# Two edits to a fused attention and two-MLP kernel: partial sums of the first MLP kept in memory, and a priority for four activations

## The chip, the cores and the metric

The kernel runs on one core of one Trainium2 chip. The metric is device time in microseconds (us) of one execution; the kernel before ran three times, 584.2, 585.54 and 586.94 us, so its median is 585.54 us. Lower is better. Engines are named as the profile does: PE is TensorE (matrix products), PEld its weight loads, DVE is VectorE, ACT is ScalarE, POOL is GpSimd, SP is SyncE, whose queue issues most of the DMAs.

## What is computed

A decaying linear attention over 2 batches of 768 positions, 8 heads of 64, gives x of 1536 tokens by 512. Two MLPs follow, each 512 to 2048 to 512; the first squares a ReLU, the second uses a leaky ReLU:

```
x = attention(q, k, v, lam)            # 1536 x 512
h = np.maximum(x @ w_in, 0.0)
x = h * h @ w_out                      # first MLP
h = x @ w2_in
g = np.maximum(0.01 * h, h)
out = g @ w2_out                       # second MLP
```

Inputs to the attention are float32. The MLP weights come as 64-bit floats.

## The kernel before, in words

**Precision by splitting.** Each MLP operand is split into a high part and a low part (`split`, `converting`, `activate`), and a product is three matrix products: high by high, high by low, low by high (`three`). Weights arrive as raw 64-bit words in `raw` (two buffers of 1 MB), and `converting` turns one such piece into a high and a low tile by steps on ACT (lines 109 and 128) and DVE (lines 110 to 130). A generator hands out one conversion step at a time between groups of products.

**Tiling and stages.** The 1536 tokens are three token tiles of 512, t = 0, 1, 2. The 2048 hidden features are cut into four pieces of 512, so each MLP l (0 or 1) has four stages s. In a stage, `first` computes the hidden features of one token tile (four blocks m of 128, 12 products each) and `activate` makes their high and low parts, `g0h`/`g0l` for t = 0, `g1h`/`g1l` for t = 1. `second` then multiplies them by the second weight matrix: four output blocks m per token tile, 12 products each, into one of eight PSUM banks.

**The pair group.** In the second MLP, token tiles 0 and 1 are done together by `first_pair`: a seven-product scheme in place of eight. Its operands are differences of token halves (`token_sums`, which writes tiles `t2`, `t3`, `t4`) and of weight halves (`weight_sums`). Per half h of the stage it runs the seven products; `plus` (line 507) adds up their results on DVE under a raised priority of 400, and `put` hands the four finished blocks of each token tile to `activate` (lines 441 to 443: two ACT operations and one DVE subtraction that writes the low part). After `first_pair`, PE goes on with `second(1, s, 0)`, which reads `g0h` and `g0l`, block by block: products 1 to 3 need block 0, 4 to 6 block 1, and so on.

**Partial sums.** Each output block gets one contribution from each of the four stages. In the first MLP they are added up on the chip in `acc[t]`, one tile of 128 x 4 x 512 for each token tile: a copy on ACT in stage 0 (line 575), an add on DVE in stages 1 and 2 (line 585), and an add in stage 3 that gives the result (line 578, or 585 for t = 2), which is split into `xhi`, `xlo`. These three tiles carry the tags t2, t3 and t4, which `token_sums` uses again for its own tiles; so a tile of `token_sums` can be written only when the `acc` tile of that tag has been read for the last time, and `acc[2]` is read until the end of the first MLP. In the second MLP they are added up in device memory: a copy on ACT into a buffer `f` (line 591), a plain DMA to `spill` in stage 0, an adding DMA issued by POOL in stages 1 and 2 (line 601), and in stage 3 the sum is loaded back and added to the last contribution on DVE (line 594). Buffers `f` come from a pool of nine (`plain`), which `activate`, `first_pair` and `token_sums` use as well.

**What sets the order.** The order on PE is the program's (a manual schedule). The orders on ACT, DVE, POOL and SP are set by a scheduler at build time, which takes the program's order and the priorities that `tc.high_priority` gives. Each engine and each queue works its list strictly in order: an instruction that waits holds all behind it.

Of the kernel before, what the change touches and what calls it, by code (L numbers as in the profile page):

```python
# [9 lines left out]
F32 = mybir.dt.float32  # L10
# [4 lines left out]
ALU = mybir.AluOpType  # L15
P = 128
# [3 lines left out]
def tile_retention_then_two_mlps(  # L20
# [12 lines left out]
    nc = tc.nc  # L33
    B, H, S, D = q.shape
    NT, DM = out.shape
# [4 lines left out]
    TT = 512  # L40
    NTILE = NT // TT
# [8 lines left out]
    dram = ctx.enter_context(tc.tile_pool(name="dram", bufs=1, space=bass.MemoryType.DRAM))  # L50
# [10 lines left out]
    def plain():  # L61
        return fp.tile([P, TT], F32, tag="f", name="f")

    def dma(dst, src):
        return nc.sync.dma_start(dst, src)  # L65

    def split(hi, lo, src):
        nc.scalar.copy(hi, src)
        nc.vector.tensor_tensor(out=lo, in0=src, in1=hi, op=ALU.subtract)
# [81 lines left out]
    xhi = [None] * NTILE  # L151
    xlo = [None] * NTILE

    def new_x(t):
        xhi[t] = xp.tile([P, KD, TT], F32R, tag=f"xhi{t}", name=f"xhi{t}")
        xlo[t] = xp.tile([P, KD, TT], F32R, tag=f"xlo{t}", name=f"xlo{t}")
# [233 lines left out]


    late = ctx.enter_context(tc.tile_pool(name="late", bufs=1, reuse_waits="tile"))
    spill = [[dram.tile([P, DM], F32, name=f"spill{t}{m}") for m in range(4)] for t in range(NTILE)]
    spilled = {}
    g, acc, x0f, x1f, tt = {}, [None] * NTILE, {}, {}, {}

    def new_g(t, first_stage=False):
        if first_stage and t == 2:
            tags = ("sw0", "sw1")
        else:  # L400
            tags = (f"g{t % 2}h", f"g{t % 2}l")
        g[t] = [late.tile([P, KF, TT], F32R, tag=tag, name=tag) for tag in tags]
# [32 lines left out]
    def activate(l, src, r, ghi, glo):  # L435
        if l == 0:
            nc.scalar.activation(r, src, AF.Relu)  # L437
            nc.scalar.square(ghi, r)
            nc.scalar.square(r, r)  # L439
        else:  # L440
            nc.scalar.activation(ghi, src, AF.Prelu, alpha=0.01)
            nc.scalar.activation(r, src, AF.Prelu, alpha=0.01)
        nc.vector.tensor_tensor(out=glo, in0=r, in1=ghi, op=ALU.subtract)  # L443
# [25 lines left out]
    def first_pair(s):  # L469
        new_g(0)  # L470
        new_g(1)
        ve = nc.vector
        w = {}
        for h in range(2):
            hi, lo = wts[1, s, 0, h]
            for i in range(2):
                for j in range(2):
                    w[h, f"A{i + 1}{j + 1}"] = [x[:, 2 * j:2 * j + 2, i * P:(i + 1) * P] for x in (hi, lo)]
            for n in range(4):
                w[h, f"S{n + 1}"] = [sums[s, h][:, part, n] for part in range(2)]  # L480
        x = {
            "B11": (xhi[0][:, 0:2], xlo[0][:, 0:2]),
            "B21": (xhi[0][:, 2:4], xlo[0][:, 2:4]),
            "B22": (xhi[1][:, 2:4], xlo[1][:, 2:4]),
            "T1": (xhi[1][:, 0:2], xlo[1][:, 0:2]),
        }
        for n in (2, 3, 4):
            x[f"T{n}"] = (tt[n][:, 0], tt[n][:, 1])
        ps, s1, s2, r22 = {}, {}, {}, {}

        def product(h, where, a, b, start=True):
            if start:
                ps[h, where] = bank()
            (ah, al), (bh, bl) = w[h, a], x[b]
            ops = []
            for j in range(2):
                ops += [(ah[:, j], bh[:, j]), (ah[:, j], bl[:, j]), (al[:, j], bh[:, j])]
            three(ps[h, where], ops, start, True, not start)
            return ps[h, where]

        def put(h, src, r, i, t):
            m = 2 * h + i
            activate(1, src, r, g[t][0][:, m], g[t][1][:, m])

        def plus(h, out, where, other):
            with tc.high_priority(offset=400):
                ve.tensor_tensor(out=out, in0=ps[h, where], in1=other, op=ALU.add)

        both = range(2)
        for h in both:  # L510
            b = product(h, "A", "A11", "B11")
            s1[h] = plain()
            nc.scalar.copy(s1[h], b)
            yield True
        for h in both:
            product(h, "B", "S2", "T2")
            s2[h] = plain()
            plus(h, s2[h], "B", s1[h])
            yield True
        for h in both:  # L520
            product(h, "D", "A22", "T4")
            yield True
        for h in both:
            product(h, "C", "S1", "T1")
            yield True
        for h in both:
            product(h, "B", "S3", "T3", False)
            plus(h, s1[h], "B", s1[h])
            r22[h] = plain()
            plus(h, r22[h], "C", s1[h])  # L530
            plus(h, s1[h], "D", s1[h])
            yield False
        for h in both:
            put(h, product(h, "A", "A12", "B21", False), plain(), 0, 0)
            put(h, s1[h], s1[h], 1, 0)
            yield False
        for h in both:
            product(h, "C", "S4", "B22", False)
            plus(h, s2[h], "C", s2[h])
            yield False  # L540
        for h in both:
            put(h, r22[h], r22[h], 1, 1)
            put(h, s2[h], s2[h], 0, 1)

    def second(l, s, t, ms=range(4)):
        last = s == NS - 1
        groups = [(m, slice(0, DM)) for m in ms]
        if (l, s, t) == (1, NS - 1, NTILE - 1):
            groups[-1:] = [(3, slice(0, DM // 2)), (3, slice(DM // 2, DM))]
        for m, cs in groups:  # L550
            if l == 0 and m == 0:
                if s == 0:
                    acc[t] = late.tile([P, 4, 512], F32, tag=f"t{t + 2}", name=f"acc{t}")
                if last:
                    new_x(t)
            if l == 1 and last and cs.start == 0:
                spilled[m] = plain()
                dma(spilled[m], spill[t][m])
            ghi, glo = g[t]
            ms_ = slice(m * P, (m + 1) * P)  # L560
            ops = []
            for kk in range(KF):
                hi, lo = (x[:, kk % 2] for x in wts[l, s, 1, kk // 2])
                if l == 0:
                    ops += [(hi[:, ms_], ghi[:, kk]), (hi[:, ms_], glo[:, kk]), (lo[:, ms_], ghi[:, kk])]
                else:
                    ops += [(ghi[:, kk, ms_], hi[:, cs]), (ghi[:, kk, ms_], lo[:, cs]), (glo[:, kk, ms_], hi[:, cs])]
            ps = bank()[:, cs]
            three(ps, ops[:6], True, False)
            yield  # L570
            three(ps, ops[6:], False, True)
            if l == 0:
                a = acc[t][:, m]
                if s == 0:
                    nc.scalar.copy(a, ps)
                elif last and t < 2:
                    f = plain()
                    nc.vector.tensor_tensor(out=f, in0=ps, in1=a, op=ALU.add)
                    (x0f, x1f)[t][m] = f
                    if t == 0 or m > 1:  # L580
                        split(xhi[t][:, m], xlo[t][:, m], f)
                    if t == 1 and m > 1:
                        token_sums(m - 2)
                else:
                    nc.vector.tensor_tensor(out=a, in0=ps, in1=a, op=ALU.add)
                    if last:
                        split(xhi[t][:, m], xlo[t][:, m], a)
            else:
                if not last:
                    spilled[m] = plain()  # L590
                    nc.scalar.copy(spilled[m], ps)  # L591
                else:
                    a = spilled[m][:, cs]
                    nc.vector.tensor_tensor(out=a, in0=ps, in1=a, op=ALU.add)
                if last:
                    r0 = t * TT + m * P
                    dma(out[r0:r0 + P, cs], spilled[m][:, cs])
                elif s == 0:
                    dma(spill[t][m], spilled[m])
                else:  # L600
                    nc.gpsimd.dma_start(spill[t][m], spilled[m], accum_op=ALU.add)  # L601
            if t == 2 and m == 3:
                i = stages.index((l, s))
                opened.update((*stages[n], 1, h) for n, h in ((i + 1, 1), (i + 2, 0)) if n < len(stages))
            yield not (l == 0 and last and t == 1 and m > 1)
# [49 lines left out]
```

## Time and profile before

| | |
|---|---|
| median of three runs | 585.54 us |
| profiled execution, its own time | 584.32 us |
| its span, first to last instruction | 582.5 us |
| PE busy | 571.4 us, 98% of the span, 3099 instructions |
| PEld busy | 476.1 us, 82% |
| DVE busy | 405.1 us, 70%, 565 instructions |
| ACT busy | 277.0 us, 48%, 425 instructions |
| POOL busy | 46.6 us, 8%, 61 instructions |
| moved by DMA | 59.75 MB, 103 GB/s in the mean |

The profile gives each group of instructions its busy time and the idle time of its engine just before it, with the engine that released it. The ends of matrix products are modelled and overlap their successors, so times between starts tell more on PE than busy time. A timeline lists instructions in order of time, equal neighbours merged (x2, x3); the bracket at the end of a row is the idle time before it and its releaser. In tile names of the profile the buffer numbers are left out: `t` stands for t2, t3 and t4, `raw<-in_moe_w_in` for the first and the second MLP's weights alike. A name such as SPq is the issuing queue of an engine.

### The profile page before, as it was taken

What the parts mean: (1) busy time and instruction counts of PE and PEld (TensorE: products, weight loads), DVE (VectorE), ACT (ScalarE), POOL (GpSimd) and SP (SyncE); (2) the same over time, 40 slices, a digit from 0 to 9 for tenths busy, and PEclk for the clock granted to TensorE, in tenths of its full rate; (3) what the DMA queues carried; (4) which work ended last, traced back from release to release, by engine and by line L of the source; (5) the groups of instructions that cost most, each with busy time, mean ns of one, the idle gap of its engine ahead of it and who ended that gap; (6) DMA issues with size and microseconds to landing.
All of it is one profiled execution on the core that took longest, in us unless ns stands there. A gap on an engine that the chain in (4) does not pass through costs nothing.

```text
span 582.5 us, 7802 instructions
## 1 busy us (share of the span) xinstructions
PE 571.4 (98%) x3099; PEld 476.1 (82%) x3099; DVE 405.1 (70%) x565; ACT 277.0 (48%) x425; POOL 46.6 (8%) x61
## 2 busy tenths in 40 slices
PE   6999999999999999999999979999999999999997
PEld 6888888888888888888888858888888888888886
DVE  3789999949248752969768999929874787316222
ACT  2344698537361661528537473633662475325110
POOL 3426000000000000000000000000203111220000
PEclk9899999999999999999999999999999999999999
DMA  8999432443104040122201215262339424562432
GB/s 175 236 206 205 159 122 95 153 136 98 47 0 132 14 145 0 61 85 73 72 1 41 82 46 191 70 214 81 45 101 237 83 60 55 69 94 55 161 110 91
DMA packets 60148, 59.75 MB, mean 103 GB/s; under 512 B 38984, under 2 KB 40272, under 8 KB 60112
## 3 DMA queue, kind: packets, MB, share of 16 engines
q1 hardware_dynamic: 56128, 52.71, 30.0%
q0 software_dynamic: 3456, 6.29, 7.9%
q8 instruction: 24, 0.39, 0.3%
q10 hardware_dynamic: 528, 0.26, 0.2%
q14 instruction: 12, 0.10, 0.1%
HBM read 46.66 MB, written 12.59 MB: 102 GB/s over the span
## 4 chain that ended last, share of the span: by engine, by line
PE 95%; DMA 2%; DVE 1%; issue 1%; SPq 0%; ACT 0%; POOL 0%; ACTq 0%; POOLq 0%
PE ps L447 88%; PE ps L268 2%; PE ps L285 2%; PE ps L336 2%; DMA raw<-in_moe_w_in 1%; PE ps L334 1%; PE ps L309 1%; DMA q<-in_q 1%; SPq L65 0%; DVE g0l L443 0%; ACT qT L272 0%; POOL kd L303 0%; DVE hb L120 0%; DVE rb L117 0%; PE ps L259 0%
## 5 line engine op out<-in xcount | busy, mean ns | idle before, releaser
L447 PE MATMUL ps<-xhi,w1h 128*128 128x512 f32 x288 | 112.1, 389 | 0.0
L447 PE MATMUL ps<-xlo,w1h 128*128 128x512 f32 x288 | 112.0, 389 | 0.0
L447 PE MATMUL ps<-xhi,w1l 128*128 128x512 f32 x288 | 112.0, 389 | 0.0
L447 PEld LDWEIGHTS ps<-xhi,w1l 128*128 128x128 f32 x288 | 54.1, 188 | 11.3
L447 PEld LDWEIGHTS ps<-xhi,w1h 128*128 128x128 f32 x288 | 54.1, 188 | 11.2 <-issue 0.2
L447 PEld LDWEIGHTS ps<-xlo,w1h 128*128 128x128 f32 x288 | 54.1, 188 | 11.2
L443 DVE TENSOR_TENSOR g0l<-f,g0h 128x512 fp32r<-128x512 f32 x60 | 41.0, 688 | 26.3 <-ACT f L439 14.9
L601 POOL DMA_DIRECT2D spill<-f x24 | 21.7, 903 | 437.0 <-ACT f L591 437.0
L447 PE MATMUL ps<-w2h,g0l 128*128 128x512 f32 (+1 forms) x132 | 50.8, 385 | 3.1 <-DVE g0l L443 3.1
L130 DVE TENSOR_TENSOR w2l<-hb,w2h 128x1024 fp32r<-128x1024 f32 x16 | 19.6, 1224 | 47.4 <-ACT w2h L128 47.2
L447 PE MATMUL ps<-w2l,g0h 128*128 128x512 f32 (+1 forms) x132 | 50.5, 383 | 0.0
L447 PE MATMUL ps<-w2h,g0h 128*128 128x512 f32 (+1 forms) x132 | 50.5, 383 | 0.0
L437 ACT ACTIVATE f<-ps 128x512 f32<-128x512 f32 x48 | 28.5, 593 | 39.5 <-PE ps L447 39.5
L591 ACT COPY f<-ps 128x512 f32<-128x512 f32 x36 | 21.1, 587 | 53.4 <-PE ps L447 51.2
L109 ACT ACTIVATE hb<-raw 128x1024 f32<-128x1024 f32 x32 | 36.8, 1154 | 16.6 <-DMA raw<-in_moe_w_in 5.6
L447 PE MATMUL ps<-g0h,w2h 128*128 128x512 f32 x112 | 43.6, 389 | 0.0
L447 PE MATMUL ps<-g0l,w2h 128*128 128x512 f32 x112 | 43.6, 389 | 0.0
L447 PE MATMUL ps<-g0h,w2l 128*128 128x512 f32 x112 | 43.6, 389 | 0.0
L117 DVE SCALAR_TENSOR_TENSOR rb<-raw,rb 128x1024 f32<-128x1024 uint32 x32 | 39.1, 1222 | 0.4
L120 DVE TENSOR_TENSOR hb<-hb,rb 128x1024 f32<-128x1024 f32 x32 | 39.1, 1222 | 0.3
L113 DVE SCALAR_TENSOR_TENSOR hb<-raw,hb 128x1024 uint32<-128x1024 uint32 x32 | 39.1, 1222 | 0.3
L128 ACT CAST w2h<-hb 128x1024 fp32r<-128x1024 f32 x16 | 16.9, 1054 | 39.2 <-PE ps L447 37.3
(125 smaller groups left out, 1106.4 us busy)
## 6 DMA issues: line engine op xcount, KB each, us to landing
raw<-in_moe_w_in SPq DMA_DIRECT2D x16, 1024.0 KB, 5.6
raw<-in_moe_w_out SPq DMA_DIRECT2D x16, 1024.0 KB, 4.8
spill<-f POOLq DMA_DIRECT2D x24, 256.0 KB, 4.3
k<-in_k SPq DMA_DIRECT2D x12, 256.0 KB, 4.9
q<-in_q SPq DMA_DIRECT2D x12, 256.0 KB, 5.1
v<-in_v SPq DMA_DIRECT2D x12, 256.0 KB, 4.9
spill<-f SPq DMA_DIRECT2D x12, 256.0 KB, 2.9
f<-spill SPq DMA_DIRECT2D x12, 256.0 KB, 2.8
```

The costliest lines, as they stand in the source:

```text
L109: nc.scalar.activation(hf, w_hi.bitcast(F32), AF.Abs)
L113: yield ve.scalar_tensor_tensor(out=hb, in0=w_hi, scalar=0xC0000000, in1=hb, op0=ALU.bitwise_and, op1=ALU.bitwise_or)
L117: yield ve.scalar_tensor_tensor(out=rf, in0=w_lo, scalar=2.0 ** -52, in1=rf, op0=ALU.mult, op1=ALU.mult)
L120: yield ve.tensor_tensor(out=hf, in0=hf, in1=rf, op=ALU.add)
L128: nc.scalar.copy(hi, hf)
L130: yield ve.tensor_tensor(out=lo, in0=hf, in1=hi, op=ALU.subtract)
L268: nc.tensor.transpose(ps[:, p, :], src[:, 2 * p:2 * p + 2, :].rearrange("s h d -> s (h d)"), ident)
L437: nc.scalar.activation(r, src, AF.Relu)
L443: nc.vector.tensor_tensor(out=glo, in0=r, in1=ghi, op=ALU.subtract)
L447: nc.tensor.matmul(ps, a, b, start=start and n == 0, stop=stop and n == len(ops) - 1, skip_group_check=again)
L591: nc.scalar.copy(spilled[m], ps)
L601: nc.gpsimd.dma_start(spill[t][m], spilled[m], accum_op=ALU.add)
```

## The change

Two edits, as the diff shows. First, the first MLP's partial sums go the way of the second's: stage 0 copies the product to a buffer `f` and writes it to `spill[0]` by a plain DMA, stages 1 and 2 copy it and add it there by an adding DMA of POOL, stage 3 loads the sum into an `f` buffer before the products and adds on DVE in place. The tiles `acc` are gone. Second, in `put` the activations of t = 0 stand under a priority of 400.

```diff
-    spill = [[dram.tile([P, DM], F32, name=f"spill{t}{m}") for m in range(4)] for t in range(NTILE)]
+    spill = [[[dram.tile([P, DM], F32, name=f"spill{l}{t}{m}") for m in range(4)] for t in range(NTILE)]
+             for l in range(2)]
...
             m = 2 * h + i
-            activate(1, src, r, g[t][0][:, m], g[t][1][:, m])
+            with tc.high_priority(offset=400 if t == 0 else 0):
+                activate(1, src, r, g[t][0][:, m], g[t][1][:, m])
...
-            if l == 0 and m == 0:
-                if s == 0:
-                    acc[t] = late.tile([P, 4, 512], F32, tag=f"t{t + 2}", name=f"acc{t}")
-                if last:
-                    new_x(t)
-            if l == 1 and last and cs.start == 0:
+            if l == 0 and last and m == 0:
+                new_x(t)
+            if last and cs.start == 0:
                 spilled[m] = plain()
-                dma(spilled[m], spill[t][m])
+                dma(spilled[m], spill[l][t][m])
...
+            if not last:
+                spilled[m] = plain()
+                nc.scalar.copy(spilled[m], ps)
                 if s == 0:
-                    nc.scalar.copy(a, ps)
-                elif last and t < 2:
-                    f = plain()
-                    nc.vector.tensor_tensor(out=f, in0=ps, in1=a, op=ALU.add)
-                    (x0f, x1f)[t][m] = f
+                    dma(spill[l][t][m], spilled[m])
+                else:
+                    nc.gpsimd.dma_start(spill[l][t][m], spilled[m], accum_op=ALU.add)
+            else:
+                a = spilled[m][:, cs]
+                nc.vector.tensor_tensor(out=a, in0=ps, in1=a, op=ALU.add)
+                if l == 1:
+                    r0 = t * TT + m * P
+                    dma(out[r0:r0 + P, cs], a)
+                elif t == 2:
+                    split(xhi[t][:, m], xlo[t][:, m], a)
+                else:
+                    (x0f, x1f)[t][m] = a
                     if t == 0 or m > 1:
-                        split(xhi[t][:, m], xlo[t][:, m], f)
+                        split(xhi[t][:, m], xlo[t][:, m], a)
                     if t == 1 and m > 1:
                         token_sums(m - 2)
...
```

On PE no instruction moves: its list is the same in both kernels. DVE has 24 instructions fewer (the adds of stages 1 and 2), ACT 24 more (the copies of the same), POOL 24 adding DMAs more, and SP 24 DMAs more (12 writes in stage 0, 12 loads in stage 3). In the changed file line 443 has become 444, 441 and 442 are 442 and 443, and 507 is 509.

**VectorE, the last conversion steps ahead of the end of the first pair group.** `t_2728` is t4; L507 and L509 are the adds of `plus`; the other rows convert weights. Before:

```order
L130 TENSOR_TENSOR w2l<-hb,w2h 128x1024
L69 TENSOR_TENSOR t_2728<-f,t_2728 128x512 x2
L120 TENSOR_TENSOR hb<-hb,rb 128x1024
L110 TENSOR_SCALAR hb<-hb 128x1024
L111 TENSOR_SCALAR hb<-hb 128x1024
L507 TENSOR_TENSOR f<-ps,f 128x512
L130 TENSOR_TENSOR w2l<-hb,w2h 128x1024
```

Now:

```order
L130 TENSOR_TENSOR w2l<-hb,w2h 128x1024
L120 TENSOR_TENSOR hb<-hb,rb 128x1024
L110 TENSOR_SCALAR hb<-hb 128x1024
L111 TENSOR_SCALAR hb<-hb 128x1024
L130 TENSOR_TENSOR w2l<-hb,w2h 128x1024
L113 SCALAR_TENSOR_TENSOR hb<-raw,hb 128x1024
```

The two writes of t4 have left this place for earlier ones, behind the `token_sums` that feed them, and one conversion step (L113) stands ahead of the adds.

**VectorE, the rows that follow: the end of the pair group, where g0l is written for PE.** Before:

```order
L507 TENSOR_TENSOR f<-ps,f 128x512 x4
L113 SCALAR_TENSOR_TENSOR hb<-raw,hb 128x1024
L507 TENSOR_TENSOR f<-ps,f 128x512 x3
L116 TENSOR_SCALAR rb<-hb 128x1024
L443 TENSOR_TENSOR g0l<-f,g0h 128x512
L117 SCALAR_TENSOR_TENSOR rb<-raw,rb 128x1024
L443 TENSOR_TENSOR g0l<-f,g0h 128x512
L120 TENSOR_TENSOR hb<-hb,rb 128x1024
L443 TENSOR_TENSOR g0l<-f,g0h 128x512 x2
L443 TENSOR_TENSOR g1l<-f,g1h 128x512 x4
```

Now:

```order
L509 TENSOR_TENSOR f<-ps,f 128x512 x6
L444 TENSOR_TENSOR g0l<-f,g0h 128x512
L509 TENSOR_TENSOR f<-ps,f 128x512
L116 TENSOR_SCALAR rb<-hb 128x1024
L444 TENSOR_TENSOR g0l<-f,g0h 128x512 x3
L509 TENSOR_TENSOR f<-ps,f 128x512
L117 SCALAR_TENSOR_TENSOR rb<-raw,rb 128x1024
L444 TENSOR_TENSOR g1l<-f,g1h 128x512
L120 TENSOR_TENSOR hb<-hb,rb 128x1024
L444 TENSOR_TENSOR g1l<-f,g1h 128x512 x3
```

Of the conversion steps only L116 stands ahead of or between the four writes of g0l now, and the last add of `plus`, which serves t = 1, stands behind them.

**SyncE's queue, stage 3 of the first MLP.** `raw` is a piece of weights; spill_999 to spill_1010 are the first MLP's twelve blocks in memory, four to a token tile. Before, these five rows followed each other:

```order
L65 DMA raw<-in_moe_w_in 128x4x256 x2
L65 DMA raw<-in_moe_w_out 128x2x512 x2
L65 DMA raw<-in_moe_w_in 128x4x256 x2
L65 DMA raw<-in_moe_w_out 128x2x512
L65 DMA spill_999<-f 128x512
```

Now:

```order
L65 DMA raw<-in_moe_w_out 128x2x512 x2
L65 DMA f<-spill_999 128x512
L65 DMA f<-spill_1000 128x512
L65 DMA f<-spill_1001 128x512
L65 DMA f<-spill_1002 128x512
L65 DMA f<-spill_1003 128x512
L65 DMA f<-spill_1005 128x512
L65 DMA f<-spill_1004 128x512
L65 DMA f<-spill_1006 128x512
L65 DMA f<-spill_1007 128x512
L65 DMA f<-spill_1008 128x512
L65 DMA f<-spill_1009 128x512
```

Twelve loads (the twelfth, spill_1010, follows) stand between the last piece of second weights and the two pieces of first weights for the second MLP's stage 1, which come right behind them. (In the list of before, spill_999 is a block of the second MLP.)

## Rows read from the trace of the kernel before

**Rows 1.** Waits of TensorE: line, what ended them; us in total, times, longest

```profile
PE ps L447 <- DVE g0l L443: 3.1, 3, 1.5
```

**Rows 2.** Busy us (instructions) by engine in two stretches, TensorE clock, DMA share, GB/s

```profile
300.00:350.00 50.00, 46.94 (x205) 37.92 (x204) 46.29 (x65) 32.14 (x50) 0.00 (x0) 1.00 0.17 53
285.00:312.00 27.00, 27.00 (x120) 22.34 (x119) 18.60 (x27) 12.97 (x20) 0.00 (x0) 1.00 0.00 1
```

**Rows 3.** Chain of waits, the piece ahead of the wait: start, us, what

```profile
63.51 280.40 PE ps L447 x1236
```

**Rows 4.** Timeline of TensorE, end of the pair group: start, us, instruction, idle before

```profile
343.73 0.39 PE L447 MATMUL ps<-w2h,g0h 128*128 128x512 f32 x1
...
345.88 0.50 PE L447 MATMUL ps<-w2h,g0l 128*128 128x512 f32 x1 [1.53 <-DVE g0l L443]
...
349.36 0.50 PE L447 MATMUL ps<-w2h,g0l 128*128 128x512 f32 x1 [0.76 <-DVE g0l L443]
...
350.15 0.40 PE L447 MATMUL ps<-w2h,g0l 128*128 128x512 f32 x1
```

**Rows 5.** Timeline of VectorE in the same place and ahead of it

```profile
332.25 1.24 DVE L130 TENSOR_TENSOR w2l<-hb,w2h 128x1024 fp32r<-128x1024 f32 x1
333.38 1.31 DVE L69 TENSOR_TENSOR t<-f,t 128x512 fp32r<-128x512 f32 x2
334.59 1.24 DVE L120 TENSOR_TENSOR hb<-hb,rb 128x1024 f32<-128x1024 f32 x1
...
343.94 0.69 DVE L507 TENSOR_TENSOR f<-ps,f 128x512 f32<-128x512 f32 x1 [0.25 <-PE ps L447]
344.54 0.69 DVE L116 TENSOR_SCALAR rb<-hb 128x1024 uint32<-128x1024 uint32 x1
...
346.88 0.69 DVE L443 TENSOR_TENSOR g0l<-f,g0h 128x512 fp32r<-128x512 f32 x1
```

**Rows 6.** Timeline of ScalarE in the same place

```profile
333.52 1.15 ACT L109 ACTIVATE hb<-raw 128x1024 f32<-128x1024 f32 x1
335.86 1.05 ACT L128 CAST w2h<-hb 128x1024 fp32r<-128x1024 f32 x1 [1.19 <-DVE hb L120]
338.99 1.16 ACT L109 ACTIVATE hb<-raw 128x1024 f32<-128x1024 f32 x1 [2.08 <-DVE w2l L130]
340.04 0.60 ACT L441 ACTIVATE g0h<-ps 128x512 fp32r<-128x512 f32 x1
...
344.03 1.18 ACT L442 ACTIVATE f<-f 128x512 f32<-128x512 f32 x2
```

**Rows 7.** Groups, VectorE, 130:300, first MLP's adds: count, busy us, mean ns, idle

```profile
L585 DVE TENSOR_TENSOR acc<-ps,acc 128x512 f32<-128x512 f32 x24 | 16.5, 689 | 19.8 <-PE ps L447 19.6
```

**Rows 8.** The page's groups, second MLP's copies

```profile
L591 ACT COPY f<-ps 128x512 f32<-128x512 f32 x36 | 21.1, 587 | 53.4 <-PE ps L447 51.2
```

**Rows 9.** Timeline of SyncE's queue, weights: first start, us over both, what

```profile
268.21 10.75 SPq L65 DMA_DIRECT2D raw<-in_moe_w_out  x2
...
316.99 14.60 SPq L65 DMA_DIRECT2D raw<-in_moe_w_in  x2
```

**Rows 10.** DMA issues by line: count, KB each, median us to landing

```profile
raw<-in_moe_w_in SPq DMA_DIRECT2D x16, 1024.0 KB, 5.6
...
f<-spill SPq DMA_DIRECT2D x12, 256.0 KB, 2.8
```

**Rows 11.** Timeline of VectorE, the last stage of the first MLP

```profile
285.35 0.69 DVE L578 TENSOR_TENSOR f<-ps,acc 128x512 f32<-128x512 f32 x1
...
312.17 0.69 DVE L443 TENSOR_TENSOR g0l<-f,g0h 128x512 fp32r<-128x512 f32 x1
```

**Rows 12.** Durations, ns min/median/max: POOL's adding DMAs; VectorE's L116, 400:520 and 130:300

```profile
L601 POOL DMA_DIRECT2D spill<-f x24: 853/862/1290, 414.6 to 517.5; - x24
L116 DVE TENSOR_SCALAR rb<-hb x6: 684/694/695, 417.4 to 495.8; 128x1024 uint32<-128x1024 uint32 x6
L116 DVE TENSOR_SCALAR rb<-hb x10: 687/689/696, 135.1 to 276.6; 128x1024 uint32<-128x1024 uint32 x10
```

More of the change, by code (lines that the diff above doesn't have):

```diff
@@ L392, in tile_retention_then_two_mlps @@
     late = ctx.enter_context(tc.tile_pool(name="late", bufs=1, reuse_waits="tile"))
-    spill = [[dram.tile([P, DM], F32, name=f"spill{t}{m}") for m in range(4)] for t in range(NTILE)]
+    spill = [[[dram.tile([P, DM], F32, name=f"spill{l}{t}{m}") for m in range(4)] for t in range(NTILE)]
+             for l in range(2)]
     spilled = {}
-    g, acc, x0f, x1f, tt = {}, [None] * NTILE, {}, {}, {}
+    g, x0f, x1f, tt = {}, {}, {}, {}
     def new_g(t, first_stage=False):
@@ L571, in second @@
             three(ps, ops[6:], False, True)
-            if l == 0:
-                a = acc[t][:, m]
+            if not last:
+                spilled[m] = plain()
+                nc.scalar.copy(spilled[m], ps)
                 if s == 0:
-                    nc.scalar.copy(a, ps)
-                elif last and t < 2:
-                    f = plain()
-                    nc.vector.tensor_tensor(out=f, in0=ps, in1=a, op=ALU.add)
-                    (x0f, x1f)[t][m] = f
+                    dma(spill[l][t][m], spilled[m])
[11 more added lines that the diff above has]
+                    (x0f, x1f)[t][m] = a
                     if t == 0 or m > 1:
-                        split(xhi[t][:, m], xlo[t][:, m], f)
+                        split(xhi[t][:, m], xlo[t][:, m], a)
                     if t == 1 and m > 1:
                         token_sums(m - 2)
[L584 to L601, printed above, removed]
             if t == 2 and m == 3:
```

## The prediction, made before the changed kernel ran

> **What bounds the kernel now.** I read the list of waits first, then the windows, the chain of waits, and the timelines of PE, DVE and ACT around the one place they lead to. PE is the bound: it is busy nearly all the time, and behind the attention its list of waits holds one entry only, three waits for g0l of together 3.1 us [rows 1]. The windows put it in 300 to 350 us: there PE is busy 46.94 of 50 us, and DVE 46.29, so DVE has hardly a gap, at a TensorE clock of 1.00 [rows 2]. The reader is to see that a change elsewhere on DVE, ACT, POOL or SP is worth nothing unless PE comes to wait for it, and that at most this one wait can be won.
>
> What it costs is read from starts, since the busy time of a product overlaps its successor. The chain of waits has 1236 products back to back in 280.40 us, 0.227 us each [rows 3]. The twelve products of the first block behind the pair group start at 343.73, the twelfth at 350.15 [rows 4]. Undisturbed it would start at 343.73 + 11 x 0.227 = 346.23. So the wait costs 3.9 us, more than the 3.1 in the list, since each of the three restarts also loses an overlap.
>
> Its cause is on DVE. The last add of `plus` waits for PE until 343.94, and from then on the list runs L116, g0l, L117, g0l, L120, g0l, g0l [rows 5]. A row of 512 columns takes 0.60 us from start to start (343.94 to 344.54), as does L116; the 1024-wide steps take 1.13 (332.25 to 333.38). So three conversion steps, 0.60 + 1.13 + 1.13 = 2.9 us, and the add of 0.60 stand ahead of the last g0l.
>
> **The change part by part.** *The priority.* In the new list six adds of `plus` run, then g0l, an add, L116, and three g0l; L117 and L120 have moved behind them. *The tiles acc are gone.* So the two writes of t4 no longer wait for acc[2]: the 1.21 us that they take at 333.38 [rows 5] leave the crowded stretch for an earlier place beside `token_sums`, and L113 (1.13) takes their room ahead of the adds. I work the new list through on the old clock, with 0.60, 1.13, and 0.69 to the end of a 512-wide step:
>
> DVE: L130 at 332.25, L120 at 333.38, done 334.6. L110 waits for ACT's L109, which starts at 333.52 as now and lasts 1.15 [rows 6]: L110 at 334.7, L111 at 335.4. The second L130 needs ACT's L128, which waits for L120 now too; it runs 334.7 to 335.75. So L130 at 336.1, L113 at 337.2, six adds from 338.4 to 342.0. Their inputs are there: the products of the fifth pair (S3 by T3) end at about 338.45, 24 products before the 343.73 of [rows 4] (343.73 - 24 x 0.227 = 338.28, and 0.17 for the last one's end).
>
> ACT: its second L109, released by L130, starts at about 337.3 in place of 338.99, so the first g0h starts as soon as its product is done, near 339.9 (now 340.04). One operation takes 0.50 (340.04 to 344.03, eight operations [rows 6]). The four pairs of operations that g0l needs are done at about 341.0, 343.7, 344.2 and 344.7.
>
> g0l: block 0 at 342.0, done 342.7. The next add needs a product that ends at 342.5, so 342.6; L116 at 343.2; block 1 at 343.8, done 344.5; blocks 2 and 3 done at 345.1 and 345.7. PE wants them for its products 3, 6, 9 and 12: 344.18, 344.87, 345.55, 346.23. All are in time, the tightest by 0.4 us. So the whole 3.9 us is won, and a slip up to 0.4 costs nothing.
>
> Neither edit does this alone. Without the priority the last add still waits for PE until 343.94 and the same rows follow it, so a DVE that is 1.2 us less late changes nothing. Without the move of t4 the priority would find DVE 1.2 us later, and PE would wait some 0.8 us for block 1.
>
> *What goes and comes elsewhere.* 24 adds of 0.689 us leave DVE, in a stretch where it stood idle 19.8 us before them [rows 7]: no gain, PE covers it. 24 copies of 0.587 us [rows 8] come to ACT, 14.1 us over two stages of some 65 us (288 products each). They replace the adds as what empties PSUM, and PE has eight banks of 2.7 us of products each to wait in: nothing. If that cover failed, each copy would cost at most its 0.59.
>
> *POOL.* 24 adding DMAs, 0.86 us of issue each [rows 12]. POOL has nothing else to do there. An `f` buffer is held until the DMA has landed.
>
> [...] The same 24 issues already run in the second MLP; L116 takes 694 ns beside them and 689 ns in the first MLP without them, and the longest of the 24 issues is 1.29 us against a median of 0.86 [rows 12]. [...]
>
> *SP.* Twelve writes in stage 0 stand in the list between pieces of weights that are wanted a stage later, and the twelve loads come behind the second of the two pieces of second weights: its issue ends at 268.21 + 10.75 = 278.96 [rows 9]. Seven loads follow at once into free buffers, the other five as buffers come free. The loads share the engines with that 1 MB piece, which lands 5.6 us later by the longer row of [rows 10], at 284.6; a load alone takes 2.8. So the first lands between 282.2 and, if it goes behind the piece, some 285.5. The first add that needs it ran at 285.35 [rows 11]. From there to 312 DVE is idle 27.00 - 18.60 = 8.4 us [rows 2], so a load that is late by a microsecond disappears in gaps. The value is 0; below 0 there is nothing to win, above it is a rival.
>
> The loads also stand ahead of the next first weights, issued at 316.99. The last load must wait for one of nine `f` buffers; counting them, it takes the one that g0l frees at 312.17 + 0.69 [rows 11], so it is out of the way 4 us early. Those weights are used by L109 at 333.52 or later [rows 6], and land at 322.6: another 10.9 us of cover.
>
> *The sum.* The profiled execution took 584.32 us; less 3.9 gives 580.4. The median of the runs shown, 585.54, lies 1.2 above it, so I expect 581.6.
>
> **The rivals.** (A) The forecast: all of it won, 581.6, between 580.2 and 583.0 with the spread of the runs.
>
> (B) Part of it. The margin is 0.4 us, and a single 1024-wide step that comes in late on DVE or ACT (1.13) leaves PE 1.13 - 0.4 = 0.7 us to wait, two of them 1.9. For it speaks that DVE has no gap in this stretch; against it that the list is fixed and its inputs were worked through. Won are 2.0 to 3.2: 582.3 to 583.5, in the middle 582.9.
>
> (C) No change, 585.5: the 3.9 us come back at the next thing that is late, so the change does not do what it says. After 349 PE waits for nothing more [rows 1], and g1l, which DVE puts off, is wanted only 96 products, 22 us, later. So there is little for it.
>
> (D) Slower: the SP queue. The first load sits behind two pieces of weights, and a late load stops DVE in its list, the adds behind it, and with them the results that free PSUM and feed the pair group. It decides from where DVE's 8.4 us of gaps are used up. If the 1.05 MB of weights and the 1.83 MB of seven loads went at the page's mean rate of 103 GB/s, the first load would land 12.7 us after 278.96, at 291.7, 6.3 late; the fourth at 299.4, the seventh at 306.9. With gaps this is just covered; without them, and some 7 us of it reaching PE, 585.54 - 3.9 + 7 = 588.6. Against it: a load alone takes 2.8 us.
>
> [...]
>
> **How the numbers follow.** A 0.58, B 0.20, C 0.12, D 0.08, E 0.02. The time is that of A, 581.6. The range goes from 580.0, a little under A's own, to 585.2: all of A and B and a third of C. A measurement of this kernel can tell about 0.5% from no change, 2.9 us, so faster begins below 582.6. A lies 1.0 under that line, and the three runs of before spread 2.7; I count 0.51 of A as faster and 0.07 as same, of B 0.07 and 0.13, of C 0.11 as same and 0.01 slower, D and E as slower. That makes faster 0.58, same 0.31, slower 0.11.
>
> **What would show it.** In the profile of the changed kernel: the entry "PE waits for g0l" gone or under 0.5 us; the twelve products behind the first pair group 0.227 us apart; on DVE six adds and g0l ahead of L116, and g0l's block 1 starting near 343.8; t4 written before 322; busy time of DVE down by 16, of ACT up by 14; POOL with 48 adding DMAs; in stage 3 no add of DVE that waits for a load. [...] A longer attention phase or a lower clock would be none of these, and would make the prediction wrong for a reason that it does not hold.

## The result and the profile after

The changed kernel took 580.64 us (median of 6 runs, 580.41 to 580.81), the kernel before 585.96 us beside it (6 runs, 584.20 to 587.41): a ratio of 0.991, with 95% between 0.9891 and 0.9929. So it is faster by 5.3 us. The forecast was 581.6 us with a range of 580.0 to 585.2; the time lies in it, 1.0 under the forecast. The profiled execution of the changed kernel took 580.56 us with a span of 578.8, so it stands at its median. That of the kernel before, from which the prediction was made, took 584.32: from profile to profile the gain is 3.8 us. The 1.5 us between 3.8 and 5.3 is the part that had to be explained.

The wait that answers to [rows 1] is gone. The whole list of TensorE's waits in the changed kernel (engine, line, what ended them; us in total, times, longest) holds the attention only:

```profile
PE ps L309 <- issue: 2.0, 1, 2.0
PE ps L194 <- POOL pw L199: 1.5, 1, 1.5
PE ps L285 <- ACT qT L272: 1.4, 2, 1.1
PE ps L268 <- DMA k<-in_k: 0.8, 1, 0.8
PE ps L309 <- ACT kT L272: 0.4, 1, 0.4
```

The chain of waits says the same from the other side. Where it had a piece of 1236 products and a break [rows 3], one piece (start, us, what) now runs from the first product of the first MLP to the last product of the kernel:

```profile
63.79 511.75 PE ps L448 x2268
```

The windows over the stretch of [rows 2], and over the six microseconds in which the wait was (stretch and its length; busy us and instructions of PE, weight load, DVE, ACT, POOL; TensorE clock, DMA share, GB/s):

```profile
300.00:350.00 50.00, 50.00 (x222) 41.40 (x222) 47.47 (x68) 32.43 (x52) 0.00 (x0) 1.00 0.24 71
...
344.00:350.00 6.00, 6.00 (x28) 4.97 (x27) 6.00 (x10) 5.26 (x11) 0.00 (x0) 1.00 0.08 21
```

PE is now busy all 50 us, and DVE is no less full than it was (47.47 us beside 46.29). The two writes of t4 have left this stretch: the last one starts at 321.9, where it started at 334.0 before, and other steps have come up into their room, in another order. TensorE's timeline shows the products of [rows 4] again: the first of the block, and the four that need a block of `g0l`.

```profile
344.01 0.39 PE L448 MATMUL ps<-w2h,g0h 128*128 128x512 f32 x1
...
344.46 0.39 PE L448 MATMUL ps<-w2h,g0l 128*128 128x512 f32 x1
...
345.14 0.39 PE L448 MATMUL ps<-w2h,g0l 128*128 128x512 f32 x1
...
345.82 0.39 PE L448 MATMUL ps<-w2h,g0l 128*128 128x512 f32 x1
...
346.50 0.39 PE L448 MATMUL ps<-w2h,g0l 128*128 128x512 f32 x1
```

Eleven products lie between 344.01 and 346.50, 0.226 us each: no wait is left. DVE's timeline, which answers to [rows 5]:

```profile
336.37 1.22 DVE L130 TENSOR_TENSOR w2l<-hb,w2h 128x1024 fp32r<-128x1024 f32 x1
337.50 1.22 DVE L113 SCALAR_TENSOR_TENSOR hb<-raw,hb 128x1024 uint32<-128x1024 uint32 x1
338.64 3.67 DVE L509 TENSOR_TENSOR f<-ps,f 128x512 f32<-128x512 f32 x6
342.23 0.68 DVE L444 TENSOR_TENSOR g0l<-f,g0h 128x512 fp32r<-128x512 f32 x1
342.85 0.69 DVE L509 TENSOR_TENSOR f<-ps,f 128x512 f32<-128x512 f32 x1
343.46 0.68 DVE L116 TENSOR_SCALAR rb<-hb 128x1024 uint32<-128x1024 uint32 x1
344.06 1.89 DVE L444 TENSOR_TENSOR g0l<-f,g0h 128x512 fp32r<-128x512 f32 x3
```

This trace runs 0.28 us later than the one before (344.01 against 343.73 for the same product). Less 0.28, the six adds start at 338.36, block 0 of `g0l` at 341.95 and block 1 at 343.78; the prediction worked out 338.4, 342.0 and 343.8.

### The profile page after: what moved, and what is told of

Same layout as the page of the kernel before. It is cut to its first block, busy times and chain, and to the rows that moved or that the text cites. A ratio compares the mean times of both kernels' runs of the same rounds, so it can differ in the third digit from the quotient of the medians.

```text
span 578.8 us, 7965 instructions
## 1 busy us (share of the span) xinstructions
PE 569.3 (98%) x3099; PEld 475.2 (82%) x3099; DVE 391.3 (68%) x541; ACT 290.1 (50%) x449; POOL 68.0 (12%) x85
## 4 chain that ended last, share of the span: by engine, by line
PE 96%; DMA 2%; DVE 1%; SPq 1%; issue 0%; ACT 0%
PE ps L448 88%; PE ps L285 2%; PE ps L336 2%; PE ps L334 2%; PE ps L268 2%; DMA k<-in_k 1%; PE ps L309 1%; SPq L65 1%; DVE pw L214 0%; DMA tab<-pw 0%; DMA sq<-in_lam 0%; DVE sq L218 0%; ACT kT L272 0%; ACT qT L272 0%; DVE f L580 0%
## 5 line engine op out<-in xcount | busy, mean ns | idle before, releaser
L577 POOL DMA_DIRECT2D spill<-f x48 | 42.9, 894 | 411.7 <-ACT f L573 411.7
L573 ACT COPY f<-ps 128x512 f32<-128x512 f32 x72 | 41.9, 585 | 98.1 <-PE ps L448 98.1
L117 DVE SCALAR_TENSOR_TENSOR rb<-raw,rb 128x1024 f32<-128x1024 uint32 x32 | 39.1, 1221 | 0.5
L113 DVE SCALAR_TENSOR_TENSOR hb<-raw,hb 128x1024 uint32<-128x1024 uint32 x32 | 39.1, 1221 | 0.4
L120 DVE TENSOR_TENSOR hb<-hb,rb 128x1024 f32<-128x1024 f32 x32 | 39.0, 1220 | 0.3
L509 DVE TENSOR_TENSOR f<-ps,f 128x512 f32<-128x512 f32 x40 | 26.2, 684 | 9.9 <-PE ps L448 9.9
```

What stands on the lines that cost most here:

```text
L113: yield ve.scalar_tensor_tensor(out=hb, in0=w_hi, scalar=0xC0000000, in1=hb, op0=ALU.bitwise_and, op1=ALU.bitwise_or)
L117: yield ve.scalar_tensor_tensor(out=rf, in0=w_lo, scalar=2.0 ** -52, in1=rf, op0=ALU.mult, op1=ALU.mult)
L120: yield ve.tensor_tensor(out=hf, in0=hf, in1=rf, op=ALU.add)
L577: nc.gpsimd.dma_start(spill[l][t][m], spilled[m], accum_op=ALU.add)
```

## The experiments

Each of them is a change to the kernel before or to the changed kernel. Its time is a median with the lowest and the highest in brackets, and its ratio is to the kernel before, run beside it.

**The priority alone.** The kernel before, with the second edit only:

```diff
-            activate(1, src, r, g[t][0][:, m], g[t][1][:, m])
+            with tc.high_priority(offset=400 if t == 0 else 0):
+                activate(1, src, r, g[t][0][:, m], g[t][1][:, m])
```

> The kernel before with the second edit alone (priority 400 for the four activations of t = 0); the sums stay on the chip. Theory 1 (the whole gain is PE's wait for g0l behind the first pair group, and the list of VectorE there decides it): with the priority the scheduler also puts L113 behind the four writes of g0l, so no conversion step is left among them though t4 is still written late. Worked through with 0.60 and 1.13 us: block 0 done at 342.0, block 1 at 344.4, blocks 2 and 3 at 345.2 and 345.8, against 344.18, 344.87, 345.55 and 346.23 wanted. So all of it is won: 580.5 to 581.2 us, no wait of PE for g0l. The prediction's side remark (block 1 some 0.8 us late) would give 581.4. Rival, theory 2 (the gain is VectorE's relief by 24 adds and the early t4): little is won, 584 to 586 us.

Measured: 580.87 us (580.15 to 581.19, 6 runs), ratio 0.9912 [0.989, 0.9933], the same as the changed kernel. The chain of waits has one piece here too, and no wait for `g0l` stands in the list. DVE's timeline:

```profile
342.51 0.69 DVE L443 TENSOR_TENSOR g0l<-f,g0h 128x512 fp32r<-128x512 f32 x1 [0.31 <-ACT f L442]
343.12 1.28 DVE L508 TENSOR_TENSOR f<-ps,f 128x512 f32<-128x512 f32 x2
344.32 0.68 DVE L443 TENSOR_TENSOR g0l<-f,g0h 128x512 fp32r<-128x512 f32 x1
344.92 0.68 DVE L508 TENSOR_TENSOR f<-ps,f 128x512 f32<-128x512 f32 x1
345.52 1.28 DVE L443 TENSOR_TENSOR g0l<-f,g0h 128x512 fp32r<-128x512 f32 x2
346.72 1.22 DVE L113 SCALAR_TENSOR_TENSOR hb<-raw,hb 128x1024 uint32<-128x1024 uint32 x1
```

The prediction took it that the conversion steps would keep their places, and that DVE would then be 1.2 us late for block 1. But the order was worked out anew: L113, which stands ahead of the adds in the changed kernel, stands behind all four `g0l` here. DVE even waits for ACT before block 0, and all blocks are in time. So the priority is enough by itself, for the whole gain, and the memory edit is not needed for it.

**The memory edit alone.** The changed kernel without the priority.

> The changed kernel without the priority: sums in memory only. Theory 1: its list of VectorE has six adds, L116, an add, L117, an add, L120 and then the four g0l together; on the changed kernel's clock the first is done at about 347.0 against 344.46 wanted, the next follow 0.60 apart where PE wants one each 0.68, so one wait of 2.5 us and 0.3 of lost overlap: 583.4 us. The prediction said that this edit alone changes nothing: 585.9. Theory 2 (VectorE's relief is the gain): near 580.6.

Measured: 584.87 us (583.19 to 587.43, 12 runs), ratio 0.998 [0.9963, 0.9997]. TensorE's wait is there, as one piece in place of three:

```profile
PE ps L448 <- DVE g0l L444: 2.4, 1, 2.4
```

On DVE the last add of `plus` does not wait for PE here. L117 stands right ahead of it, L120 behind it, and then come the four `g0l` together:

```profile
345.00 0.69 DVE L508 TENSOR_TENSOR f<-ps,f 128x512 f32<-128x512 f32 x1
...
346.74 2.50 DVE L444 TENSOR_TENSOR g0l<-f,g0h 128x512 fp32r<-128x512 f32 x4
```

The wait is the expected one, but the median is 1.5 us above the 583.4 that were expected. The timeline of TensorE shows something else behind the wait:

```profile
347.48 0.50 PE L448 MATMUL ps<-w2h,g0l 128*128 128x512 f32 x1 [2.44 <-DVE g0l L444]
...
348.51 0.62 PE L448 MATMUL ps<-w2h,g0h 128*128 128x512 f32 x1
348.93 0.63 PE L448 MATMUL ps<-w2l,g0h 128*128 128x512 f32 x1
...
351.48 0.60 PE L448 MATMUL ps<-w2l,g0h 128*128 128x512 f32 x1
351.91 0.40 PE L448 MATMUL ps<-w2h,g0l 128*128 128x512 f32 x1
```

From 348.51 to 351.48 the products start 0.42 us apart in place of 0.23, with no wait between them. The window over them:

```profile
348.00:352.00 4.00, 4.00 (x12) 3.10 (x12) 4.00 (x9) 1.52 (x3) 0.00 (x0) 0.57 0.38 157
```

PE is busy all the time with 12 products, where the changed kernel runs 20 in the same stretch at a clock of 1.00. Taken by single microseconds, the granted clock was 0.76 from 348, 0.50 from 349 and from 350, 0.54 from 351, and 1.00 from 352. So this wait cost twice: once while PE stood, and once behind it.

**The priority for the first group only.** The changed kernel, with `t == 0 and s == 0` in place of `t == 0`. The first group is the pair group; this asks whether the 1.5 us come from the later groups.

> The changed kernel with the priority in the first pair group only (stage 0 of the second MLP), not in the three later groups. Theory 1: the first group holds the whole wait, so 580.6 us, with the changed kernel's spread of 0.4 us over its runs. Rival, theory 3 (the runs of before spread from 584.2 to 587.4 and the median fell by 5.3 where the one wait is 3.9, so the later groups have waits that come in some executions, which the priority takes away too): 581 to 583 us with a spread of 1 to 3 us.

Measured: 580.84 us (580.44 to 582.66, 6 runs), ratio 0.9917 [0.9894, 0.994]. The later groups give nothing that the times show. One of the six runs took 582.66; it has no profile, and its cause stays open.

**The kernel before, run as a kernel of its own**, to see how far one program differs from itself:

> The kernel before, unchanged, for a second profile and more times. Theory 1: 584 to 587 us, and PE's list of waits has again 3.1 us for g0l behind the first pair group (3.9 by starts). Theory 3: if this execution is above 585.5 us, its profile shows further waits of PE for g0l in the later pair groups, 1 to 3 us together. A rival to that: the extra time lies in the attention phase (first products of the first MLP later than 63.4 us) or in a longer wait at the first group.

Measured: 585.17 us (584.31 to 587.46, 12 runs), ratio 0.9989 [0.9973, 1.0006]. Its profiled execution took 584.75, with the waits of [rows 1] and a clock of 1.00 behind them. A program that spreads over 3 us, where the changed kernel spreads over 0.4, does not do the same in each execution. That made a clock that falls in some of them the theory to test.

**The memory edit alone, with the wait filled.** The kernel of the second experiment, and twelve products into a bank that nobody reads, placed behind the pair group where PE would wait:

```diff
+    def fill():
+        ps = bank()
+        for n in range(12):
+            nc.tensor.matmul(ps, wts[1, 0, 0, 0][0][:, 0, 0:P], xhi[0][:, 0], start=n == 0, stop=n == 11)
+        yield False
...
-            parts = [first_pair(s)]
+            parts = [first_pair(s)] + ([fill()] if s == 0 else [])
```

> The kernel of e2 (sums in memory, no priority) with twelve idle products on TensorE, written to a PSUM bank that nobody reads, between the first pair group and the products that wait for g0l; they take 12 x 0.227 = 2.7 us, about the wait of e2. The output is unchanged. Theory A (what e2 lost beyond its wait, and what spreads the runs of before over 4 us, is TensorE's granted clock, which in the profile of e2 falls from 1.00 to 0.50 just behind the wait, 348.5 to 351.9 us, since the engine stood still): busy in the same time, it keeps its clock, so 580.6 + 2.7 = 583.3 us, runs within 1 us of each other, and a clock of 1.00 there. Rival B (the spread comes from DMA or from VectorE): median 584.9 and a spread of 3 to 4 us as in e2, or more, since the idle products stand in the way.

Measured: 583.07 us (582.82 to 583.88, 12 runs), ratio 0.9962 [0.995, 0.9974]. The same steps stand in DVE's list and PE has more to compute, yet the median is 1.8 us lower than without the idle products (1.5 lower when each of the two is set against the kernel before, run beside it), and its runs lie within 1.1 us. The twelve products, and the clock behind them:

```profile
344.56 2.88 PE L549 MATMUL ps<-xhi,w1h 128*128 128x512 f32 x12
...
348.00:352.00 4.00, 4.00 (x19) 3.31 (x18) 4.00 (x8) 1.67 (x3) 0.00 (x0) 1.00 0.45 182
```

With PE kept at work there is no fall in this execution: the clock of this window is 1.00, where it was 0.57 without the idle products.

**The kernel before filled.** The same in the kernel before, with 17 products, 3.86 us of them, as long as its wait costs:

> The kernel before with seventeen idle products (17 x 0.227 = 3.9 us) between the first pair group and the products that wait for g0l, written to a PSUM bank that nobody reads; the output is unchanged and VectorE's list is that of before. Theory A (beyond its 3.9 us the wait costs a fall of TensorE's clock in part of the executions): 580.6 + 3.9 = 584.4 us, within 1 us over its runs, where the kernel before spreads from 583.4 to 588.1 beside it. Rival B: median 585.7 to 586 and the spread of before.

Measured: 584.37 us (583.87 to 585.70, 12 runs) beside 585.63 (584.20 to 587.23, 17 runs) for the kernel before, ratio 0.9979 [0.9967, 0.9992]. The wait is paid in full, in products, and still 1.3 us are won. The window behind them:

```profile
350.00:354.00 4.00, 4.00 (x19) 3.27 (x18) 4.00 (x9) 0.79 (x2) 0.00 (x0) 1.00 0.62 246
```

Two of the twelve runs took 585.6 and 585.7. They have no profile, and with them the runs spread over 1.8 us, where 1 was expected.

**The kernel before, profiled four times more** (executions b, c, d and e). If the clock is the cause, some profiles of this one program must show the fall and be slower by it.

> The kernel before, unchanged, one more profile. Theory A: if its time is above 585.3 us, the granted clock of TensorE is 0.50 for some 3 us right behind the three waits for g0l and the products there are 0.42 us apart; if it is below 584.8, the clock stays 1.00 there. Rival B: a slow execution has the clock at 1.00 there and loses its time elsewhere, in the attention phase or in the later groups.

> The kernel before, unchanged, one more profile, to see one of its slow executions. Theory A: above 585.3 us the granted clock is 0.50 for 3 us or more behind the wait; below 584.8 it is 1.00 there.

> As e10: above 585.3 us a clock of 0.50 for 3 us or more behind the wait, below 584.8 a clock of 1.00 there.

> As e10: above 585.3 us a clock of 0.50 for 3 us or more behind the wait, below 584.8 a clock of 1.00 there.

With the profile shown ahead of the prediction and that of the kernel before run as its own (a) these are six executions of one program. The last three columns are the time, the start of the first product of the first MLP in the chain of waits, and their difference, in which the attention ahead has no part:

```
execution      clock behind the wait   time     start   difference
b              1.00                    583.85   63.08   520.8
shown          1.00                    584.32   63.51   520.8
a              1.00                    584.75   63.99   520.8
d              0.50, from 347.9        585.22   63.60   521.6
c              0.50, from 350.0        586.19   63.77   522.4
e              0.50, from 350.1        586.42   64.05   522.4
changed kernel 1.00, no wait           580.56   63.79   516.8
```

The starts differ by up to 1.0 us, so a part of the spread lies in the attention. The rest goes with the clock: five of the six are as theory A has them, and d, at 585.22, lies between its two bounds. There the clock fell at the second wait already, and the third wait was 0.25 us in place of 0.76, so a part of the slow products ran in time in which PE would have stood. In none of the six does PE wait for `g0l` in the later groups, so nothing speaks for theory 3.

The chain of waits from the product on with which PE goes on after its last wait, for executions b and e:

```profile
348.92 229.86 PE ps L447 x1024
```

```profile
349.91 231.44 PE ps L447 x1024
```

The same 1024 products take 1.58 us longer. The windows of e show where:

```profile
344.00:350.00 6.00, 2.93 (x11) 1.47 (x10) 5.75 (x9) 4.96 (x10) 0.00 (x0) 1.00 0.23 52
...
350.00:354.00 4.00, 4.00 (x11) 3.17 (x12) 4.00 (x9) 0.59 (x1) 0.00 (x0) 0.57 0.62 248
```

In the first window PE does 2.93 us of work in 6. In the second it is busy throughout and gets 11 products done, against 19 in execution b. In all three executions with a fall PE stood just before it, and in the two filled kernels, where idle products take the place of the wait, the clock was 1.00 in the windows behind them. In b, a and the one shown the same waits passed without a fall. So that it is the wait which brings the fall is an inference from these runs, and no trace shows how.

For runs without a profile the record has the mean granted clock of the whole run. Of the 69 runs of the kernel before that were taken beside these experiments, the 24 with a mean clock of 0.991 or less have a median of 586.6 us, and the 24 with 0.996 or more one of 584.6. None of the 42 runs without this wait (the changed kernel, the priority alone or for the first group only, and the two filled kernels) has a mean clock under 0.993. The mean takes in the start of the attention, where the clock differs between executions as well (over the first 20 us 0.91 in the profile shown ahead of the prediction, 1.00 in that of the changed kernel). But that does not show in the times: the runs of the changed kernel have means from 0.996 to 1.000 and stay within 0.4 us.

**Where the first MLP's outputs are kept.** The prediction said that the early write of t4, which the memory edit allows, changes nothing without the priority. Two kernels without the priority tell it apart. In the one only the third token tile is added up in memory, so acc[2] is gone and t4 is written early:

```diff
+            kept = l == 0 and t < 2
...
```

(The lines left out keep `acc` for the tiles for which `kept` holds.)

> Sums in memory for token tile 2 alone, those of tiles 0 and 1 on the chip, no priority. So t4 is written early, and 8 of the 24 adds have left VectorE. Its list ends with L116, three adds, L117, g0l, L120, three g0l. Theory 1, by the prediction's claim that the last add waits for PE whatever stands ahead: the add at 343.94, L117 at 344.5, block 0 done at 346.4 against 344.18 wanted, block 1 at 348.1, so PE loses 2.2 + 1.0 us and an overlap each, 3.4 us: 584.0 us without a fall of the clock, up to 585.6 with one, and the same as the next kernel (t = 2 on the chip) within 0.5 us. Theory 2 (an early t4 by itself relieves the place): 1.2 us faster than the next kernel.

The other is its mirror, `kept = l == 0 and t == 2`: the third tile stays on the chip, and t4 waits for it as before.

> The mirror of the run before: sums in memory for token tiles 0 and 1, that of tile 2 on the chip, no priority. t4 is written late, its two steps of together 1.21 us stand in the crowded stretch; the end of VectorE's list is the same as there. Theory 1: the same time as e7 within 0.5 us, 584.0 to 585.6. Theory 2: 1.2 us slower than e7.

Measured: 585.13 us (583.80 to 586.82, 10 runs) and 585.11 us (584.20 to 586.24, 10 runs), ratios 0.9994 [0.9977, 1.0012] and 0.9995 [0.998, 1.0011]. They are the same within the noise, and the same as the kernel before. Each profile has the same list of waits for `g0l`, 2.8 us in two pieces. What sets the two profiled times apart, 583.80 and 585.18, is again the clock behind the wait. From the product on with which PE goes on after its last wait, the first:

```profile
348.24 230.52 PE ps L448 x1027
```

and the second, with a clock of 0.58 from 348 to 352:

```profile
348.02 232.12 PE ps L448 x1027
```

## Why the prediction was right

**The bound and its price.** PE was the bound, and the one wait behind the attention was what was won, with the clock that hung on it. By the table the time from the first product of the first MLP to the end fell from 520.8 to 516.8 us where the clock stayed up: 4.0 us, against 3.9 in the sum, which was read from starts, and 3.1 in the list of waits. This step held, and so did the reading behind it, that the wait costs more than its idle time.

**The new list on DVE, and its margin.** It came out to within 0.1 us at the six adds, at block 0 and at block 1. On ACT the first `g0h` came near the predicted 339.9:

```profile
340.13 0.60 ACT L442 ACTIVATE g0h<-ps 128x512 fp32r<-128x512 f32 x1 [1.34 <-PE ps L448]
```

which is 339.85 on the old clock. Block 1 is done at 344.74 (it starts at 344.06, and one such step takes 0.68), and its product runs at 345.14: a margin of 0.4 us, as predicted. But the prediction looked at the products alone. The weight load of that product reads the same block (in the kernel before the loads wait for `g0l` as the products do, 1.95, 1.20 and 1.20 us), and it starts earlier:

```profile
344.92 0.19 PEld L448 LDWEIGHTS ps<-w2h,g0l 128*128 128x128 f32 x1
```

So only 0.2 us were left before this load, and that "a slip up to 0.4 costs nothing" is not shown. Rival B, a part of the gain, is refuted by the empty list.

**What was costed at nothing.** The adding DMAs, the copies and the loads cost nothing that the times show: the changed kernel, with them, and the priority alone, without them, differ by 0.2 us. The margin on the SP queue was thin, inside the prediction's own bounds. The two pieces of second weights, the twelve loads and the next first weights on that queue (first start, us over all, what):

```profile
268.45 10.79 SPq L65 DMA_DIRECT2D raw<-in_moe_w_out  x2
...
279.41 34.06 SPq L65 DMA_DIRECT2D f<-spill  x12
...
317.22 0.38 SPq L65 DMA_DIRECT2D raw<-in_moe_w_in  x1
```

From 270 to 320 us a load took 5.3 us from issue to landing by its median, where the loads of the second MLP took 2.8 [rows 10]:

```profile
f<-spill SPq DMA_DIRECT2D x12, 256.0 KB, 5.3
```

The first load took 5.2 us and landed near 284.6. The first add that needs one ran at 285.6 (285.35 before [rows 11]), 1.0 us later, and no add of that stage waited for a DMA. Rival D, the late load, is refuted: the loads are later, but not late. The last one is issued by 313.5, 3.7 us ahead of the next weights, where 4 was predicted. POOL's adding DMAs (count: lowest, median, highest ns, first and last start):

```profile
L577 POOL DMA_DIRECT2D spill<-f x48: 853/862/1237, 154.7 to 513.8; - x48
```

and L116 in the first MLP:

```profile
L116 DVE TENSOR_SCALAR rb<-hb x10: 685/687/695, 135.4 to 276.9; 128x1024 uint32<-128x1024 uint32 x10
```

Its median is 687 ns here, beside these DMAs, and was 689 ns there before, without them [rows 12]. E, the slower kernel that the prediction gives 0.02, stood for time that DVE loses beside POOL's issues. No run shows such a loss: PE waits for nothing outside the attention. But the long issues that the prediction noted have a pattern. Two of the four of the first MLP over 1.1 us, and the steps that DVE begins while they run:

```profile
177.51 1.17 POOL L577 DMA_DIRECT2D spill<-f  x1 [13.80 <-ACT f L573]
179.17 1.24 POOL L577 DMA_DIRECT2D spill<-f  x1 [0.49 <-ACT f L573]
```

```profile
177.80 0.79 DVE L110 TENSOR_SCALAR hb<-hb 128x1024 f32<-128x1024 f32 x1
...
179.65 0.68 DVE L111 TENSOR_SCALAR hb<-hb 128x1024 uint32<-128x1024 uint32 x1
```

The other two, and the two of 1.28 and 1.29 us in the kernel before, have a TENSOR_SCALAR step that begins inside them as well, 0.3 to 0.5 us after their start. The issue then takes 0.3 to 0.4 us more than its median; the step takes its usual 0.69 us, or 0.1 more. DVE's step began second in all six and took 0.79 us at most. What makes the issue longer is not shown.

DVE's busy time fell by 13.8 us (16 predicted), ACT's rose by 13.1 (14 predicted), and neither shows in the time. Rival C, a new wait in the place of the old one, has none in the list or in the chain.

**What was mis-sized: the clock.** The sum took 3.9 us off the median of the kernel before and wrote "The median of the runs shown, 585.54, lies 1.2 above it, so I expect 581.6". That carried the 1.2 over to the changed kernel, as if it were a spread that both share. The 1.0 us by which the time came out under the forecast is this term. It was not: half of six executions of the kernel before have a clock that falls behind the wait, and lose 0.8 or 1.6 us by it. The execution that the prediction read is one of the other half, at a clock of 1.00. With the wait this loss goes as well; the changed kernel's median and profile agree within 0.1 us. So the gain is the wait, 4.0, and what the clock cost the median of before, some 1.3 us. This 1.3 is a difference, 5.3 less 4.0. The idle products give back as much in the kernel before (1.3) and 1.5 to 1.8 in the one with the memory edit, but the six profiles show 0.7 in the mean: the rest of it is argued, from the mean clocks of the slower runs.

**What was wrong beside it.** "Neither edit does this alone" is wrong for the priority, which does all of it. The sentence "Without the move of t4 the priority would find DVE 1.2 us later, and PE would wait some 0.8 us for block 1" fell with the first experiment: the order found another place for L113. The sentence between the two, that without the priority "the last add still waits for PE until 343.94 and the same rows follow it", is wrong for the memory edit as it stands: there the last add starts at 345.00 behind L117 and waits for nothing, one wait of 2.44 us stands in place of three, and the median is 1.1 us lower (584.87 beside 586.01), by an interval that hardly leaves out no change. In the two kernels that have a part of the memory edit the last add does wait for PE, 0.31 and 0.32 us, with t4 early or late, and they take the same time; so the early t4 by itself is worth nothing, as the prediction said.

**What stays open.** Runs of the kernel before at 587 to 588 us, 8 of the 69, were never caught in a profile; they lie up to 1.7 us above the slowest one here, 586.42. Their mean clocks are 0.990 to 0.993, and since the mean takes in the attention too, this does not tell how long the clock stayed down behind the wait. Nor is it shown why the same program with the same waits has the fall in one execution and not in the next.

## What to carry to other kernels

Where the bound engine waits for the last step of a chain on a full engine, look at the order on that engine before the amount of work on it: here the priority alone won the whole gain (5.1 us by itself, 5.3 for both edits), and the memory edit, with 13.8 us less work on DVE, nothing that can be told on top of it. Price such a wait by the starts on both sides of it, and then look at the clock behind it, in more than one execution, before a median is set beside a single profile. A statement on what a scheduler will do without one of two edits needs the order of that kernel itself, not the order of another.

## What the hardware showed that was not expected

Short waits of TensorE were followed by a lower clock in three of six executions of the kernel before. In the kernel before the three waits are 1.53, 0.78 and 0.76 us long with products between them; in those three the granted clock fell to 0.50 some 0.2 to 0.4 us behind the end of the second or the third of them, and was back at 1.00 some 3.4 us later (worked out from windows of one microsecond). The products in execution e start 0.43 us apart in that stretch:

```profile
349.91 0.64 PE L447 MATMUL ps<-w2h,g0l 128*128 128x512 f32 x1 [0.76 <-DVE g0l L443]
350.34 0.63 PE L447 MATMUL ps<-w2h,g0h 128*128 128x512 f32 x1
...
353.66 0.39 PE L447 MATMUL ps<-w2h,g0l 128*128 128x512 f32 x1
```

The fall costs 1.6 us there, 40% of the 4.0 that the waits themselves cost. With seventeen products that nobody reads in place of the waits, the clock was 1.00 there in the execution that was profiled, and the median 1.3 us lower.
